# Gated mix of attention with memory and a gated feed-forward block: the last 256 output columns stored as two transfers, two weight loads issued in halves

## The chip, the cores and the metric

The kernel runs on one core of a Trainium2 chip. The metric is the device time of one execution in microseconds, the median of several runs. TensorE is called PE here, VectorE DVE, ScalarE ACT, GpSimd POOL and SyncE SP; SP issues nearly all DMA transfers.

## The reference

Sizes: 2048 tokens of width 512, 32 heads of 16, 4 segments of 512 tokens, 1792 hidden columns in the feed-forward block. All inputs and the output are bf16.

```python
def reference(A_x, A_wq, A_wk, A_wv, A_wo, A_beta, B_x, B_W_gate, B_W_up, B_W_down, gate_w):
    x = A_x
    g = _sigmoid((x * gate_w).sum(-1, keepdims=True))
    a = _A_ref(x, A_wq, A_wk, A_wv, A_wo, A_beta)   # attention in each segment + memory of the earlier ones, then @ wo
    b = _B_ref(x, B_W_gate, B_W_up, B_W_down)       # (relu(x @ W_gate) * (x @ W_up)) @ W_down
    return g * a + (1 - g) * b
```

## The kernel before, in words

The work goes over four segments of 512 tokens. For each segment `project` makes queries, keys and values, `attend` computes the scores, their exponentials and the attended values, `memory` adds to the running memory, and `ffn` computes the feed-forward block. `ffn` ends in 128-row pieces of output: 14 products with the down weight `wd_sb` (7 in a step named `D`, 7 in a step named `DB`) and 4 products with the output weight `wo_sb` (step `W`) go into one PSUM bank `rb`; a step `OS` scales the bank by the token's gate into an SBUF tile, on ACT or DVE; a step `ST` on SP stores it to HBM.

Every piece of work is a `Step` with an engine, a cost and the steps that it comes after. The order of the steps on each engine is written out in the table `ORDER`: each number is step number times 5 plus an index into `ENGINES` (PE, ACT, DVE, POOL, SP's queue), so the last digit's class names the engine, and only the order among numbers of one class matters. `lay_out` merges the five queues into one program; the framework then adds semaphore waits for data and for buffers.

The transfers of SP take eight semaphores in turn, DMAHW0 to DMAHW7. A transfer waits until the eighth transfer before it, which used the same semaphore, has landed. At the very end of the program SP waits for all of them and for the last steps of DVE and ACT, in five wait instructions of two semaphores each, in this order: (DMAHW3, DMAHW2), (DMAHW4, DMAHW1), (DMAHW5, DMAHW0), (DMAHW6, DVE), (DMAHW7, ACT). A barrier of all engines follows. The page shows all of these under line L1001.

The down weight (1792 KB, `ld["wd"]`, L363) and the output weight (512 KB, `ld["wo"]`, L364) are each loaded by one transfer through the helper `dma` (shown at L324).

The last 128 rows of the last segment are done by `last_rows` (L842) in three column groups: 256, 128 and 128 columns. Each has its own products (L852, L860) and its own scaling (L869 on ACT for the first two, L871 on DVE for the third). The scaled columns go into two 256-column tiles, `osbh[0]` and `osbh[1]` (named `rg` in the trace, because they are the first halves of two `rg` buffers). Two stores follow (L877): one for columns 0 to 255, issued after the first scaling, and one for columns 256 to 511, issued after the second and the third.

```python
            if h != 1:
                def sto(e, s, z=min(h, 1)):
                    nc.sync.dma_start(out=outf[tt * P:(tt + 1) * P, 2 * P * z:2 * P * z + 2 * P], in_=osbh[z])
                add(f"ST{seg}3", {"QSP": 0.4}, sto, after=dmas[-2:], prio=0.0)
```

Of the kernel before, what the change touches and what calls it, by code (L numbers as in the profile page):

```python
# [99 lines left out]
]  # L100
T0, TU, SPAN, PEN_D, PEN_A, PEN_P = 19.0, 15.6, 4.1, -23.0, 150.0, 146.0


PORT = {'TG', 'RN', 'RC', 'OA', 'KO', 'MB', 'MQ', 'MN', 'GS', 'PQ', 'PK', 'N1', 'N2', 'N3', 'NM'}
PIECE = {'MK': 0.445, 'TL': 0.22, 'ZE': 0.24, 'YL': 0.22, 'MB': 0.3}


class Step:
    pass

# [102 lines left out]
def kernel(  # L213
# [108 lines left out]
    def dma(eng, o, i, after=(), prio=0.0, kb=512, lat=3.0, name="dma"):  # L322
        key = {"SP": nc.sync, "ACT": nc.scalar, "POOL": nc.gpsimd}[eng]
        return add(name, {"Q" + eng: kb / 365.0}, lambda e, s: key.dma_start(out=o, in_=i),  # L324
                   after=[e_q, *after], prio=prio, lat=lat)

    def rows(ap, c0=None, c1=None):
        v = ap.rearrange("(c p) n -> p c n", p=P)
        return v if c0 is None else v[:, :, c0:c1]
# [676 lines left out]
```

## Time and profile before

| | |
|---|---|
| median of 3 runs | 266.98 us (266.53 to 267.01) |
| span of the profiled execution | 265.0 us |
| what the median has beyond that span | 1.98 us |
| PE busy | 258.1 us (97%) |
| ACT, DVE, POOL busy | 189.7, 181.0, 143.7 us |
| granted TensorE clock | 1.000 |
| HBM read, written | 8.26 MB, 2.10 MB |

The span runs from the first to the last instruction of the profiled execution. No other time of this execution is recorded, so the measured time of a run is set beside it: the start and end of an execution that the span leaves out are taken as the 1.98 us of the table. Busy times of different engines overlap and are not to be added.

### The profile page before, as it was taken

What the parts mean: (1) busy time and instruction counts of PE and PEld (TensorE: products, weight loads), DVE (VectorE), ACT (ScalarE), POOL (GpSimd) and SP (SyncE); (2) the same over time, 40 slices, a digit from 0 to 9 for tenths busy, and PEclk for the clock granted to TensorE, in tenths of its full rate; (3) what the DMA queues carried; (4) which work ended last, traced back from release to release, by engine and by line L of the source; (5) the groups of instructions that cost most, each with busy time, mean ns of one, the idle gap of its engine ahead of it and who ended that gap; (6) DMA issues with size and microseconds to landing.
All of it is one profiled execution on the core that took longest, in us unless ns stands there. A gap on an engine that the chain in (4) does not pass through costs nothing.

```text
span 265.0 us, 7943 instructions
## 1 busy us (share of the span) xinstructions
PE 258.1 (97%) x3293; PEld 121.0 (46%) x3337; DVE 181.0 (68%) x449; ACT 189.7 (72%) x185; POOL 143.7 (54%) x328
## 2 busy tenths in 40 slices
PE   7999999999999999999999999999999999999995
PEld 5444443545444444434444445454544444444554
DVE  1589788897774538855896476688878367666911
ACT  3699799987868786887777686886766576767012
POOL 8038978782826641378758464366468156064010
DMA  6978680426501000030403110000023100031002
GB/s 197 314 166 264 149 288 3 71 74 89 79 4 37 25 2 2 20 82 1 104 2 82 25 42 2 0 4 2 2 61 87 42 20 2 0 81 23 0 2 79
DMA packets 33422, 16.77 MB, mean 63 GB/s; under 512 B 20074, under 2 KB 33386, under 8 KB 33386
## 3 DMA queue, kind: packets, MB, share of 16 engines
q1 hardware_dynamic: 33098, 16.00, 24.3%
q8 instruction: 26, 0.43, 0.7%
q10 hardware_dynamic: 288, 0.26, 0.3%
q14 instruction: 10, 0.08, 0.1%
HBM read 8.26 MB, written 2.10 MB: 39 GB/s over the span
## 4 chain that ended last, share of the span: by engine, by line
PE 94%; DMA 1%; DVE 1%; issue 1%; ACT 1%; SPq 0%
PE rb L894 36%; PE rb L928 17%; PE rb L477 11%; PE sp L735 9%; PE rb L783 7%; PE rb L941 5%; PE rb L519 4%; DMA wv_sb<-in_A_wv_dram 1%; PE rb L678 1%; PE rb L852 1%; PE rb L502 1%; DVE hT L913 1%; ACT E L746 1%; PE rb L632 1%; PE rb L860 0%
## 5 line engine op out<-in xcount | busy, mean ns | idle before, releaser
L746 ACT ACTIVATE E<-sp 128x2048 bf16<-128x2048 f32 x72 | 135.1, 1877 | 35.0 <-PE sp L735 32.8
L756 POOL TENSOR_SCALAR_AFFINE_SELECT E<-E 64x256 bf16<-64x256 bf16 x256 | 112.3, 438 | 82.2 <-ACT E L746 68.7
L894 PE MATMUL rb<-xT,wg_sb 128*128 128x512 bf16 x216 | 55.4, 380 | 0.4
L894 PE MATMUL rb<-xT,wu_sb 128*128 128x512 bf16 x208 | 54.9, 380 | 0.8
L913 DVE TENSOR_TENSOR hT<-rb,rg 128x512 bf16<-128x512 f32 x56 | 38.2, 686 | 20.1 <-PE rb L894 14.1
L928 PE MATMUL rb<-wd_sb,hT 128*128 128x512 bf16 x198 | 48.6, 380 | 0.8 <-issue 0.2
L894 PEld LDWEIGHTS <-wg_sb 128*128 128x128 bf16 x224 | 20.7, 98 | 24.8 <-issue 3.1
L894 PEld LDWEIGHTS <-wu_sb 128*128 128x128 bf16 x224 | 20.1, 98 | 23.5 <-issue 4.5
L735 PE MATMUL sp<-QT,KT 16*64 16x320 bf16 (+7 forms) x512 | 30.3, 295 | 0.0
L735 PE MATMUL sp<-QT,KTo 32*64 32x320 bf16 (+7 forms) x512 | 30.3, 295 | 0.0
L928 PEld LDWEIGHTS <-hT 128*128 128x128 bf16 x210 | 19.4, 98 | 23.8 <-issue 3.2
L801 DVE STREAM_TRANSPOSE tA<-rb 128x512 f32<-128x512 f32 x32 | 21.9, 700 | 12.0 <-PE rb L783 11.6
L906 ACT ACTIVATE rg<-rb 128x512 bf16<-128x512 f32 x36 | 21.3, 598 | 10.1 <-PE rb L894 7.1
L735 PEld LDWEIGHTS <-KT 16*64 16x64 bf16 x512 | 10.5, 102 | 27.5 <-issue 26.9
L908 DVE TENSOR_SCALAR rg<-rb 128x512 bf16<-128x512 f32 x20 | 13.8, 688 | 7.5 <-PE rb L894 7.3
L783 PE MATMUL rb<-E,Vs 64*32 64x448 bf16 (+7 forms) x512 | 18.8, 284 | 0.0
L783 PE MATMUL rb<-E,Vp 64*32 64x448 bf16 (+7 forms) x512 | 18.4, 284 | 0.0
L950 ACT ACTIVATE osb<-rb,ngcol 128x512 bf16<-128x512 f32 x8 | 5.5, 691 | 16.2 <-PE rb L941 16.2
L952 DVE TENSOR_SCALAR osb<-rb,ngcol 128x512 bf16<-128x512 f32 x7 | 5.2, 750 | 16.1 <-PE rb L941 15.9
L477 PE MATMUL rb<-xT,wq_sb 128*128 128x512 bf16 x63 | 16.1, 380 | 0.0
L812 DVE TENSOR_TENSOR o<-tA,co 128x256 bf16<-128x256 f32 x32 | 15.4, 493 | 0.2
L477 PE MATMUL rb<-xT,wk_sb 128*128 128x512 bf16 x59 | 15.4, 379 | 0.2
(97 smaller groups left out, 298.3 us busy)
## 6 DMA issues: line engine op xcount, KB each, us to landing
out_dram<-osb SPq DMA_DIRECT2D x15, 128.0 KB, 1.8
wd_sb<-in_B_W_down_dram SPq DMA_DIRECT2D x1, 1792.0 KB
wg_sb<-in_B_W_gate_dram SPq DMA_DIRECT2D x3, 512.0 KB, 6.3
wu_sb<-in_B_W_up_dram SPq DMA_DIRECT2D x3, 512.0 KB, 6.0
Vs<-Vp SPq DMA_DIRECT2D x8, 144.0 KB, 3.2
wk_sb<-in_A_wk_dram SPq DMA_DIRECT2D x2, 256.0 KB, 3.9
wq_sb<-in_A_wq_dram SPq DMA_DIRECT2D x2, 256.0 KB, 4.7
wo_sb<-in_A_wo_dram SPq DMA_DIRECT2D x1, 512.0 KB, 4.2
```

What stands on the lines that cost most here:

```text
L477: nc.tensor.matmul(rb[s.bank][:], lhsT=w[:, ci, c * P:(c + 1) * P], rhs=xT[i][:, ci, :], start=(ci == 0), stop=(ci == NC - 1))
L735: nc.tensor.matmul(sp[64 * h:64 * h + 64, j, off:off + m], lhsT=kt[32 * j:hi, c0 + w, 64 * ck:64 * ck + 64], rhs=QT[i][32 * j:hi, c0 + w, ...
L746: nc.scalar.activation(Er[n % NE][:], sp[:], ACT.Exp, scale=SCALE)
L756: nc.gpsimd.affine_select(out=v, in_=v, compare_op=ALU.is_ge, fill=0.0, base=0, pattern=[[0, 4], [1, 64]], channel_multiplier=-1)
L783: nc.tensor.matmul(rb[s.banks[h]][32 * j:32 * j + 32, q0:q0 + m], lhsT=v[64 * h:64 * h + 64, ck // 2, o:o + 32], rhs=Er[(base + f) % NE][6 ...
L801: nc.vector.transpose(tA[k].rearrange("p b w -> p (b w)"), rb[a.banks[r]][:])
L812: nc.vector.tensor_tensor(o16[u % 2][:, :, r, :], tA[k][:, :, 0:DH], cos[k][:, :, None].to_broadcast([P, NB, DH]), ALU.mult)
L894: nc.tensor.matmul(rb[s.bank][:], lhsT=w[:, ci, fv * P:(fv + 1) * P], rhs=xT[i][:, ci, :], start=(ci == 0), stop=(ci == NC - 1))
L906: nc.scalar.activation(rgb[k][:], rb[a.bank][:], ACT.Relu)
L908: nc.vector.tensor_scalar(rgb[k][:], rb[a.bank][:], 0.0, None, ALU.max)
L913: nc.vector.tensor_tensor(hT[:, fv, :], rb[a.bank][:], rgb[k][:], ALU.mult)
L928: nc.tensor.matmul(rb[b][:], lhsT=hT[:, fv, lc:lc + P], rhs=wd_sb[:, fv, :], start=(fv == 0), stop=False)
```

## The change

Three edits. The stores of the last rows become three: columns 0 to 255 as before, columns 256 to 383 after the second scaling, and columns 384 to 511 after the third. The loads of the down and of the output weight are each issued as two transfers back to back inside the same step, the first half and the second half of the 128-row blocks of the weight. `ORDER` gets one number for the new store step (5544), and later numbers rise by 5; the three numbers at its head change places, but they belong to three different engines (79 SP, 81 ACT, 135 PE), so no engine's order changes by it.

```diff
-    79, 81, 135, 140, 160, 150, 146, 170, 167, 350, 157, 176, 355, 375, 380, 385, 390, 190, 180, 397, 360, 196, 365,
+    135, 81, 79, 140, 160, 150, 146, 170, 167, 350, 157, 176, 355, 375, 380, 385, 390, 190, 180, 397, 360, 196, 365,
...
+    def halves(eng, o, i, n, prio, kb):
+        a = dma(eng, o[:, 0:n], i[:, 0:n], prio=prio, kb=kb)
+        key = {"SP": nc.sync, "ACT": nc.scalar}[eng]
+
+        def both(e, s):
+            for h in range(2):
+                key.dma_start(out=o[:, h * n:h * n + n], in_=i[:, h * n:h * n + n])
+        a.emit = both
+        return a
...
-    ld["wd"] = dma("SP", wd_sb[:], rows(B_W_down), prio=7, kb=1792)
-    ld["wo"] = dma("SP", wo_sb[:], rows(A_wo), prio=8)
+    ld["wd"] = halves("SP", wd_sb[:], rows(B_W_down), NF // 2, 7, 1792)
+    ld["wo"] = halves("SP", wo_sb[:], rows(A_wo), NC // 2, 8, 512)
...
-            dmas.append(osl)
-            if h != 1:
-                def sto(e, s, z=min(h, 1)):
-                    nc.sync.dma_start(out=outf[tt * P:(tt + 1) * P, 2 * P * z:2 * P * z + 2 * P], in_=osbh[z])
-                add(f"ST{seg}3", {"QSP": 0.4}, sto, after=dmas[-2:], prio=0.0)
+            def sto(e, s, h=h, c0=c0, c1=c1):
+                nc.sync.dma_start(out=outf[tt * P:(tt + 1) * P, c0:c1],
+                                  in_=osbh[min(h, 1)][:, c0 % (2 * P):c0 % (2 * P) + c1 - c0])
+            add(f"ST{seg}3", {"QSP": 0.4}, sto, after=[osl], prio=0.0)
```

Between the two programs the line numbers differ by 11 or 12 from the helper on. Apart from line numbers and from the names of the DMA semaphores, which shift by up to three places, ACT, DVE and POOL have the same instructions in the same order. PE has the same instructions too, and two of its matmuls get a wait more.

SP's queue at the end of the program, before; `osb` and `rg` are the SBUF tiles that are stored, and what a transfer waits for stands in brackets:

```order
L336 DMA_TRANSPOSE memT<-mtok 128x4x128 [waits DMAHW7_49]
L955 DMA out_dram<-osb_150 128x512 [waits DMAHW0_49,DVE_49]
L955 DMA out_dram<-osb_149 128x512 [waits DMAHW1_49,Activation_49]
L955 DMA out_dram<-osb_151 128x512 [waits DMAHW2_49,Activation_49]
L877 DMA out_dram<-rg_146 128x256 [waits DMAHW3_49,Activation_49]
L877 DMA out_dram<-rg_147 128x256 [waits DMAHW4_49,DVE_49,Activation_49]
L1001 UNCONDITIONAL_BRANCH
```

The same place in the changed program:

```order
L348 DMA_TRANSPOSE memT<-mtok 128x4x128 [waits DMAHW1_49]
L966 DMA out_dram<-osb_150 128x512 [waits DMAHW2_49,DVE_49]
L966 DMA out_dram<-osb_149 128x512 [waits DMAHW3_49,Activation_49]
L966 DMA out_dram<-osb_151 128x512 [waits DMAHW4_49,Activation_49]
L887 DMA out_dram<-rg_146 128x256 [waits DMAHW5_49,Activation_49]
L887 DMA out_dram<-rg_147 128x128 [waits DMAHW6_49,Activation_49]
L887 DMA out_dram<-rg_147 128x128 [waits DMAHW7_49,DVE_49]
L1012 UNCONDITIONAL_BRANCH
```

One store has become two, and with two more transfers far ahead of it the last store now holds DMAHW7 where it held DMAHW4. The five closing wait instructions name the same pairs in the same order in both programs, so the last store's semaphore stands in the fifth of them and no longer in the second.

SP's queue where the down weight (`wd_sb`) and the output weight (`wo_sb`) are loaded, before; `pK` is the transposed key tile of the first segment:

```order
L324 DMA wd_sb<-in_B_W_down_dram 128x14x512 [waits DMAHW6_49]
L336 DMA_TRANSPOSE pK<-pkT_145 128x4x128 [waits DMAHW0_49,DMAHW7_49,DVE_49,PE_49]
L336 DMA_TRANSPOSE pK<-pkT_144 128x4x128
L324 DMA wo_sb<-in_A_wo_dram 128x4x512 [waits DMAHW1_49]
L336 DMA_TRANSPOSE pK<-pkT_144 128x4x128 [waits DMAHW2_49,DVE_49,PE_49]
```

And after:

```order
L335 DMA wd_sb<-in_B_W_down_dram 128x7x512 [waits DMAHW6_49]
L335 DMA wd_sb<-in_B_W_down_dram 128x7x512 [waits DMAHW7_49]
L348 DMA_TRANSPOSE pK<-pkT_145 128x4x128 [waits DMAHW0_49,DVE_49,PE_49]
L348 DMA_TRANSPOSE pK<-pkT_144 128x4x128 [waits DMAHW1_49]
L335 DMA wo_sb<-in_A_wo_dram 128x2x512 [waits DMAHW2_49]
L335 DMA wo_sb<-in_A_wo_dram 128x2x512 [waits DMAHW3_49]
L348 DMA_TRANSPOSE pK<-pkT_144 128x4x128 [waits DMAHW4_49,DVE_49,PE_49]
```

Each weight takes two places in the queue, ahead of the same transposes. The two matmuls of PE that get a wait more are the first to read the second half of each weight.

110 rows, old and new, of the table ORDER are left out of this document.

## The prediction

> **What bounds the kernel now.** I read the page's head and its chain of waits first, to see whether the middle of the program has room in which the two split weight loads could matter.
>
> ```profile
> span 265.0 us, 7943 instructions
> PE 258.1 (97%) x3293; PEld 121.0 (46%) x3337; DVE 181.0 (68%) x449; ACT 189.7 (72%) x185; POOL 143.7 (54%) x328
> PE 94%; DMA 1%; DVE 1%; issue 1%; ACT 1%; SPq 0%
> ```
>
> PE is busy for 97% of the span and makes 94% of the chain. Its instructions and their order stay as they are, so nothing between about 6 us and the last matmul can shrink by this change; it can only grow, where a weight came late. What is left is the tail behind the last matmul. I read it in the chain of waits from 261 us on, then in the timeline and in the lines of the two last stores (L877), of the scaling before them (L869) and of the closing waits (L1001).
>
> ```profile
> 261.82 0.24 PE rb L860 x4
> 262.08 0.35 DVE rg L871
> 262.49 0.33 SPq L877 DMA_DIRECT2D out_dram<-rg  x1
> L877 SPq EVENT_SEMAPHORE  x2: 17/352/687, 260.9 to 261.8; - x2
> DMA to landing us min/median/max: 1.5/1.5/1.5
> L1001 SPq EVENT_SEMAPHORE  x5: 28/28/28, 263.0 to 264.2; - x5
> SPq L1001 <- DMA out_dram<-rg: 1.0, 1, 1.0
> ```
>
> The last product ends at 262.06, DVE scales it by 262.43 (262.08 + 0.35), SP issues the last store at 262.49, and it lands 1.5 us later, at about 264.0. SP sits for 1.0 us in the closing waits for it. The span ends at 265.0. So the last 3 us hold a DVE step of 0.35, a store of 1.5 and a second of semaphores and barrier, one behind the other, with no engine working beside them. A saving there goes straight into the time, and a loss too.
>
> **The change part by part.** Durations come from the profiled execution, of 265.0 us from first to last instruction; the median of 266.98 has 1.98 us around that span, which I take as unchanged.
>
> First, the closing waits. The lines of L1001 on SP, asked for a stretch around the landing (263.9 to 264.3) and then for two narrow ones (264.02 to 264.05 and 264.21 to 264.24):
>
> ```profile
> L1001 SPq EVENT_SEMAPHORE  x4: 28/28/28, 264.0 to 264.2; - x4
> L1001 SPq EVENT_SEMAPHORE  x1: 28/28/28, 264.0 to 264.0; - x1
> L1001 SPq EVENT_SEMAPHORE  x1: 28/28/28, 264.2 to 264.2; - x1
> ```
>
> Of the five, one was done at 263.0; four run after the landing. The first of these four is the one that held DMAHW4, the last store's semaphore, and three more follow it, the fourth starting between 264.21 and 264.24, the first between 264.02 and 264.05: 0.16 to 0.22 us for three, so about 0.063 each. In the changed program the last store holds DMAHW7, which stands in the fifth wait. The four ahead of it ask for transfers that landed earlier, and the newest of those is the middle store. It can be issued when ACT has finished its second scaling:
>
> ```profile
> L869 ACT ACTIVATE rg<-rb,ngcol x2: 367/420/473, 260.9 to 261.5; 128x256 bf16<-128x256 f32 x1, 128x128 bf16<-128x128 f32 x1
> L877 SPq DMA_DIRECT2D out_dram<-rg x2: 332/332/332, 261.4 to 262.5; - x2
> ```
>
> The second scaling ends near 261.83 (261.46 + 0.37; the two together are 0.93 us from 260.90). The first store occupies SP until 261.73 (261.40 + 0.33). So the middle store issues at about 261.86 and lands by about 263.4, half a microsecond before the last one. The three waits are then over when the last store lands: **0.19 us** saved (0.16 to 0.22).
>
> Second, the issue of the last store. Before, one separate wait instruction of 687 ns on SP held DVE's semaphore and DMAHW4 together, and the store followed it: 262.49 against 262.43, 0.06 us after DVE ended. The first store has its data wait on the transfer itself and started at 261.40, where ACT ended at 261.37:
>
> ```profile
> 260.90 0.47 ACT L869 ACTIVATE rg<-rb,ngcol 128x256 bf16<-128x256 f32 x1 [0.58 <-PE rb L860]
> ```
>
> That is 0.03 us. The new last store waits only for DVE and DMAHW7, and like the first one it can carry the data wait itself: **0.03 us** saved. What could spoil it is SP's extra store ahead of it: issued at 261.86 it occupies SP until 262.19, and with some 0.1 us for the next wait SP stands ready at about 262.3, 0.13 us before DVE ends. So the cover holds; if ACT were late by 0.2 us, the last store would be late by 0.07.
>
> Third, the store itself becomes smaller: 128 rows of 256 bytes instead of 128 rows of 512. No store of this width is in the trace. Rows near to it are the stores of the page, by size, and the DMA share while the packets of the last store ran:
>
> ```profile
> out_dram<-osb SPq DMA_DIRECT2D x15, 128.0 KB, 1.8
> out_dram<-rg SPq DMA_DIRECT2D x2, 64.0 KB, 1.5
> Vs<-Vp SPq DMA_DIRECT2D x8, 144.0 KB, 3.2
> 260.30:261.90 1.60, 1.60 (x28) 1.52 (x25) 0.00 (x0) 0.86 (x3) 0.00 (x0) 1.00 0.72 246
> 263.20:263.70 0.50, 0.00 (x0) 0.00 (x0) 0.00 (x0) 0.00 (x0) 0.00 (x0) 1.00 0.44 131
> ```
>
> In the last row the 16 DMA engines are busy for 0.44 of 0.50 us, which is 0.22 us each for 8 rows of 512 bytes, 0.027 us a row. The row above moves 246 GB/s x 1.60 us = 394 KB at 1 KB a row, 385 rows or 24 for each engine, in 1.60 x 0.72 = 1.15 us: 0.048 a row. Carrying the line on, a row of 256 bytes takes 0.027 - 0.021 / 2 = 0.017 us, and 8 of them 0.13 instead of 0.22: 0.09 saved. From 128 KB to 64 KB the landing fell by 0.3, so half of that, 0.15, is what a size proportional to bytes gives. I take **0.10 us**, nearer to the packets' own time. The ends are a gain of 0.3 (the whole step from 1.8 to 1.5 once more) and a loss of 1.7 (if short rows make it as slow as the slowest short-row transfer of the page, Vs<-Vp with 3.2).
>
> The Trainium skill speaks against this part: the page DMA: Bandwidth & Descriptors, in its Specifications, puts the smallest transfer at line rate at 512 bytes, with a read-modify-write below it. No run here shows it yet, since all stores of this kernel have at least 512 bytes a row. By it the third term would be a loss and not a gain; two of the rivals are what that does.
>
> Fourth, the two split loads:
>
> ```profile
> 32.87 0.57 SPq L324 DMA_DIRECT2D wd_sb<-in_B_W_down_dram  x1
> 46.96 3.30 SPq L336 DMA_TRANSPOSE pK<-pkT  x2
> 50.31 0.58 SPq L324 DMA_DIRECT2D wo_sb<-in_A_wo_dram  x1
> 56.73 3.35 SPq L336 DMA_TRANSPOSE pK<-pkT  x2
> 38.00:40.00 2.00, 2.00 (x10) 0.77 (x8) 1.81 (x4) 2.00 (x4) 0.94 (x3) 1.00 0.88 309
> 40.00:42.00 2.00, 2.00 (x17) 0.92 (x17) 2.00 (x6) 1.57 (x2) 1.79 (x4) 1.00 0.00 1
> L928 PE MATMUL rb<-wd_sb,hT x198: 378/379/390, 63.4 to 255.9; 128*128 128x512 bf16 x198
> wo_sb<-in_A_wo_dram SPq DMA_DIRECT2D x1, 512.0 KB, 4.2
> L941 PE MATMUL rb<-wo_sb,oT x7: 379/379/389, 81.7 to 83.2; 128*128 128x512 bf16 x7
> ```
>
> Each adds one issue of 0.6 us to SP. Behind the down weight SP's next work starts at 46.96, 13.5 us after 33.44; behind the output weight at 56.73, 5.8 us after 50.89. Both issues vanish in these gaps; without the gaps they would cost the transposes of `pK` 0.6 us each. The down weight has landed by 40 (the DMA share falls from 0.88 to nothing) and is first read at 63.4; the output weight lands at 54.5 and is first read at 81.7. Twenty-three and twenty-seven microseconds cover any way of cutting them. On the critical engine two matmuls get a wait on a semaphore that has long been there. The batch at 81.7 begins with a matmul that already carries such a wait: its longest is 389 ns against a median of 379, so at most 0.01 us each; I take nothing, with 0.02 lost as the bound.
>
> The two transfers more also shift which transfer each later one has to wait for, but only to ones that landed long before. For instance the two transfers that follow the output weight and the transposes of `pK` (the third segment's input and the first load of `Vs`, in the 60s of the span) now ask for the halves of the down weight, landed by 40.
>
> Sum: 0.19 + 0.03 + 0.10 = **0.32 us** less, a span of 264.7 and a median of 266.98 - 0.32 = **266.66 us**, 0.12% less.
>
> **The rivals.** *The store's landing shrinks by a whole step.* If the fall from 1.8 to 1.5 repeats, the third term is 0.30 and the sum 0.52: 266.46, at the edge of 0.2%. For it speaks that the two page rows have only their size between them; against it, that the packets of the last store take 0.22 us in all, so more than that can't come from fewer bytes. Chance 0.15.
>
> *The short rows give the gain back.* If each row of 256 bytes takes another pass, a read and then a write, the packets' time of 0.22 doubles: the landing becomes 1.72, the third term a loss of 0.22, and the sum 0.19 + 0.03 - 0.22 = 0: 266.98. This is the mild form of the skill's rule above. Against it speaks that the line from 1024 to 512 bytes shows nothing but a smaller cost. Chance 0.13.
>
> *Slower: the last store waits for a slow write.* The mechanism is the same place, the one transfer that nothing covers, but with a full round trip to memory ahead of its writes, so that it lands like Vs<-Vp in 3.2 us instead of 1.5: 266.98 - 0.22 + 1.7 = 268.46. It decides as soon as the landing is over 1.5 + 0.22 + 0.53 = 2.25 us. Against it: rows of 512, 576 and 1024 bytes are all there, and Vs<-Vp differs by more than width (256 pieces on 64 partitions, between two SBUF tiles). Chance 0.06.
>
> That the change doesn't do what it says is not open: the order shows the last store on the fifth wait.
>
> **How the numbers follow.** A measurement of this kernel can tell about 0.2%, 0.53 us, from no change: the three runs before differ by 0.48. The forecast has the chance 0.66 that is left. Its own bounds are a third term of 0 to 0.15 and a first of 0.16 to 0.22: 266.58 to 266.83; the runs' spread, 0.24 to either side, widens that to 266.3 to 267.1. This holds the first two rivals as well, nearly whole, and I take 266.25 to 267.10. Faster by over 0.2% (below 266.45): 0.6 of the first rival and, by spread, 0.2 of the forecast, together 0.22. Slower (above 267.51): the third rival, 0.06, and 0.01 by spread: 0.07. Within 0.2%: 0.71.
>
> **What would show it.** In the profile after, the last store's DMAHW7 wait should be the only closing wait that ends after the landing, with one drain directly behind it. The middle store should issue at about 0.5 us after the first, the last at 0.03 us after DVE, and its landing should read 1.4. The first reads of both weights should start where they did, at 63.4 and 81.7, within 0.1. The forecast is wrong if the landing is over 1.6, if the last store issues after DVE by 0.1 or more, or if PE's last matmul ends over 0.3 us earlier or later than 262.06: then something in the middle moved, for which I have no cause.

## The result and the profile after

| | before | after |
|---|---|---|
| median | 266.98 us (266.53 to 267.58, 17 runs) | 266.58 us (266.31 to 267.29 and one of 299.43, 17 runs) |
| after to before | | 0.9984, 95% interval 0.9976 to 0.9992 |

The change saves 0.16%, 0.4 us, with an interval from 0.2 to 0.6 us. The run of 299.43 us, the profiled one, had a granted clock of 0.853; ratio and interval leave it out, and the lines below come from a second profile of the same program at full clock (run *again* below). First the head of its page and its chain of waits at the end, which answer to the lines shown of before:

```profile
span 265.6 us, 7945 instructions
PE 259.0 (98%) x3293; PEld 121.6 (46%) x3337; DVE 181.0 (68%) x449; ACT 189.7 (71%) x185; POOL 143.8 (54%) x328
```

```profile
262.60 0.24 PE rb L872 x4
262.84 0.02 issue
262.86 0.35 DVE rg L883
```

This span is longer than that of before, 265.6 against 265.0, and its last product ends at 262.84 instead of 262.06. So PE's last product lies 0.78 us later in this execution, and the tail behind it is shorter. The two have to be read apart. The tail first: its timeline, the lines of the last stores (now L887), of the closing waits on SP (now L1012, asked for three stretches) and the sizes of the transfers.

```profile
262.18 1.39 SPq L887 DMA_DIRECT2D out_dram<-rg  x3
```

```profile
L887 SPq EVENT_SEMAPHORE  x3: 17/17/17, 261.7 to 263.0; - x3
L887 SPq DMA_DIRECT2D out_dram<-rg x3: 332/333/350, 262.2 to 263.2; - x3
DMA to landing us min/median/max: 1.5/1.5/1.5
```

```profile
L1012 SPq EVENT_SEMAPHORE  x3: 28/28/28, 263.6 to 263.8; - x3
L1012 SPq EVENT_SEMAPHORE  x1: 28/28/28, 264.1 to 264.1; - x1
...
L1012 SPq EVENT_SEMAPHORE  x1: 28/28/28, 264.7 to 264.7; - x1
L1012 SPq DRAIN  x1: 13/13/13, 264.8 to 264.8; - x1
```

```profile
out_dram<-rg SPq DMA_DIRECT2D x2, 32.0 KB, 1.5
```

The separate wait (EVENT_SEMAPHORE) in front of the last store is 17 ns instead of 687: the store holds its data wait itself and starts at 263.24, 0.03 us after DVE's end at 263.21. Three of the closing waits are over at 263.8, the fourth at 264.1, when the middle store has landed, and only the fifth runs at 264.72, when the last store has; the drain, SP's next instruction, follows it at 264.78. Before, the drain came 0.25 us after the first wait behind the landing (264.29 against 264.04):

```profile
L1001 SPq DRAIN  x1: 7/7/7, 264.3 to 264.3; - x1
```

### The profile page after: what moved, and what is told of

It reads as the page before. It is cut to its first block, busy times and chain, and to the rows that moved or that the text cites. A ratio compares the mean times of both kernels' runs of the same rounds, so it can differ in the third digit from the quotient of the medians.

```text
span 297.7 us, 7945 instructions
## 1 busy us (share of the span) xinstructions
PE 290.2 (97%) x3293; PEld 128.3 (43%) x3337; DVE 180.9 (61%) x449; ACT 191.0 (64%) x185; POOL 143.9 (48%) x328
## 4 chain that ended last, share of the span: by engine, by line
PE 96%; issue 1%; DMA 1%; DVE 1%; DVEq 0%
PE rb L905 38%; PE rb L939 18%; PE rb L489 11%; PE sp L747 9%; PE rb L795 7%; PE rb L952 5%; PE rb L531 4%; PE rb L514 1%; PE rb L690 1%; PE rb L864 1%; DMA xT<-in_A_x_dram 1%; PE rb L644 1%; PE rb L402 1%; PE rb L872 0%; DVE hT L924 0%
## 5 line engine op out<-in xcount | busy, mean ns | idle before, releaser
L905 PE MATMUL rb<-xT,wg_sb 128*128 128x512 bf16 x216 | 63.0, 421 | 0.6
L905 PE MATMUL rb<-xT,wu_sb 128*128 128x512 bf16 x208 | 61.9, 420 | 1.2
L939 PE MATMUL rb<-wd_sb,hT 128*128 128x512 bf16 x198 | 55.5, 420 | 1.1 <-issue 0.2
L905 PEld LDWEIGHTS <-wg_sb 128*128 128x128 bf16 x224 | 22.2, 104 | 29.8 <-issue 3.3
L905 PEld LDWEIGHTS <-wu_sb 128*128 128x128 bf16 x224 | 21.5, 104 | 27.6 <-issue 4.7
L795 PE MATMUL rb<-E,Vs 64*32 64x448 bf16 (+7 forms) x512 | 20.8, 303 | 0.0
L795 PE MATMUL rb<-E,Vp 64*32 64x448 bf16 (+7 forms) x512 | 20.4, 304 | 0.0
L489 PE MATMUL rb<-xT,wq_sb 128*128 128x512 bf16 x63 | 18.1, 416 | 0.0
L489 PE MATMUL rb<-xT,wk_sb 128*128 128x512 bf16 x59 | 17.5, 423 | 0.3
L952 PE MATMUL rb<-wo_sb,oT 128*128 128x512 bf16 x58 | 16.3, 422 | 0.2
```

Source lines behind the costliest of these rows:

```text
L489: nc.tensor.matmul(rb[s.bank][:], lhsT=w[:, ci, c * P:(c + 1) * P], rhs=xT[i][:, ci, :], start=(ci == 0), stop=(ci == NC - 1))
L795: nc.tensor.matmul(rb[s.banks[h]][32 * j:32 * j + 32, q0:q0 + m], lhsT=v[64 * h:64 * h + 64, ck // 2, o:o + 32], rhs=Er[(base + f) % NE][6 ...
L905: nc.tensor.matmul(rb[s.bank][:], lhsT=w[:, ci, fv * P:(fv + 1) * P], rhs=xT[i][:, ci, :], start=(ci == 0), stop=(ci == NC - 1))
L939: nc.tensor.matmul(rb[b][:], lhsT=hT[:, fv, lc:lc + P], rhs=wd_sb[:, fv, :], start=(fv == 0), stop=False)
L952: nc.tensor.matmul(rb[hold.bank][:], lhsT=oT[i][:, ci, lc:lc + P], rhs=wo_sb[:, ci, :], start=False, stop=(ci == NC - 1))
```

## The experiments

Runs of the same program differ in when PE begins its long middle part, so two distances are compared besides the times: from the first product with the down weight to the last product of the program (the middle), and from the end of DVE's last step to the end of the span (the tail). All are from the records of the profiled executions, in microseconds. For stores_only and loads_only the landing of the last store is not recorded; it is read from the closing wait that it ends, which in the others starts 0.02 us after the landing.

| kernel | first down product | middle | tail | landing of the last store | waits behind it | time to before, 95% interval |
|---|---|---|---|---|---|---|
| before | 63.40 | 198.42 | 2.62 | 1.53 | 3 | 1 |
| again | 64.19 | 198.42 | 2.34 | 1.46 | 0 | 0.9987 (0.9972 to 1.0002) |
| again2 | 63.65 | 198.42 | 2.34 | 1.46 | 0 | 0.9991 (0.9981 to 1.0000) |
| stores_only | 63.88 | 198.42 | 2.43 | 1.44 | 2 | 0.9988 (0.9976 to 1.0000) |
| loads_only | 63.37 | 198.43 | 2.50 | 1.53 | 1 | 0.9997 (0.9986 to 1.0009) |
| pad_only | 63.39 | 198.42 | 2.45 | 1.53 | 0 | 0.9990 (0.9981 to 1.0000) |
| first_wait | 63.16 | 198.42 | 2.61 | 1.49 | 4 | 1.0000 (0.9988 to 1.0012) |
| last64 | 63.61 | 198.50 | 2.61 | 1.46 | 0 | 0.9987 (0.9978 to 0.9997) |
| warm24 | 63.94 | 198.51 | 2.32 | 1.46 | 0 | 0.9994 (0.9983 to 1.0005) |

**The changed kernel twice more** (no edit).

> The changed kernel itself, for a profile at full clock and a second comparison. Theory (only the tail moved): PE's last matmul ends within 0.1 us of the 262.06 of before; the last store issues 0.03 us after DVE ends (before 0.06), lands 1.47 us later (before 1.53 to 1.55), and only one closing wait ends after the landing. Span 264.7 to 264.8, time 0.30 us under before. Rival (the split loads moved the middle): PE's last matmul ends more than 0.1 us earlier than 262.06, and the tail accounts for less than the whole gain.

> The changed kernel once more, beside warm24 on the same chip. Theory: 0.28 us under before (2.62 - 2.34 behind DVE's end), ratio 0.999, and the first down product anywhere between 63.1 and 64.2, with 198.42 us from it to the last product. Rival (something in the middle moved after all): that distance differs by more than 0.02.

The tail came out as the theory has it both times: 2.34 us instead of 2.62, a gain of 0.28. The middle is 198.42 us, the same as before to the last digit. What failed is the expectation on the place of the last product: it lies 0.78 and 0.25 us later than before. Since the middle is unchanged, that shift arises ahead of the first down product, and it is there in kernels that are alike in that part of the program; the last experiment turns to it. The span of 264.7 was therefore missed (265.6 and 265.0). The times are 0.13% and 0.09% under before, but both intervals reach no change, so these two runs alone do not show the gain; that of the result does.

**The stores alone.** Both weights are loaded whole:

```diff
-    ld["wd"] = halves("SP", wd_sb[:], rows(B_W_down), NF // 2, 7, 1792)
-    ld["wo"] = halves("SP", wo_sb[:], rows(A_wo), NC // 2, 8, 512)
+    ld["wd"] = dma("SP", wd_sb[:], rows(B_W_down), prio=7, kb=1792)
+    ld["wo"] = dma("SP", wo_sb[:], rows(A_wo), prio=8)
```

> The three stores alone; both weights are loaded by one transfer each as before. The last store then holds DMAHW5, the third of the five closing waits. Theory: two waits of 0.063 us follow the landing, so 0.06 of the 0.19 us of the first term is left, with 0.04 from the earlier issue and 0.07 from the smaller store: 0.17 us under before, and from DVE's end to the span's end 2.44 us (2.615 before). Rival (the middle carries the gain): as fast as the changed kernel in the tail, and at the time of before where the loads mattered.

The closing waits of this kernel between 264.3 and 264.6, the landing being at 264.37:

```profile
L1012 SPq EVENT_SEMAPHORE  x3: 28/28/28, 264.4 to 264.5; - x3
```

The first of the three holds the last store, two follow, and the tail is 2.43 against 2.44 expected. Without the two split loads the smaller store gives only 0.19 of the 0.28 us.

**The loads alone.** Before, with the two weights in halves and the two stores as they were:

```diff
-    ld["wd"] = dma("SP", wd_sb[:], rows(B_W_down), prio=7, kb=1792)
-    ld["wo"] = dma("SP", wo_sb[:], rows(A_wo), prio=8)
+    ld["wd"] = halves("SP", wd_sb[:], rows(B_W_down), NF // 2, 7, 1792)
+    ld["wo"] = halves("SP", wo_sb[:], rows(A_wo), NC // 2, 8, 512)
```

> The two split loads alone, with the two stores of before. The last store (256 columns) then holds DMAHW6, the fourth closing wait. Theory: one wait follows the landing, two fewer than before: 0.13 us under before, all behind the landing; issue 0.06 us after DVE and landing 1.53 as before; PE's last matmul within 0.1 us of 262.06. Rival (the split loads move the middle): a gain of 0.2 us or more, and PE's last matmul earlier by that.

Its closing waits from 263.9 to 264.1:

```profile
L1011 SPq EVENT_SEMAPHORE  x2: 28/28/28, 264.0 to 264.1; - x2
```

One wait follows the landing; the tail is 2.50, 0.12 less than before, and issue and landing are those of before (0.06 and 1.53). The middle, which begins with the first use of the split weight, did not move. The loads themselves are issued ahead of it, at 33 to 51 us; the stretch from PE's first product with `wk_sb` (8 to 9 us) to the first down product, which holds them, took 55.15 us here, 55.13 in before, and 55.13 in the seven others. The time itself, 0.9997 with 0.1% to either side, can't tell 0.12 us from none; the tail can.

**Other counts of transfers.** *pad_only* is before with the down weight in two and the output weight in three transfers, so that the old store comes to the fifth wait; *first_wait* is the changed kernel with both weights in four transfers, so that the new store comes to the first. With a helper `parts_of` that issues the pieces between given cuts (the helper and the lines replaced are left out here):

```diff
# pad_only, against before
+    ld["wd"] = parts_of("SP", wd_sb[:], rows(B_W_down), (0,7,14), 7, 1792)
+    ld["wo"] = parts_of("SP", wo_sb[:], rows(A_wo), (0,2,3,4), 8, 512)
# first_wait, against the changed kernel
+    ld["wd"] = parts_of("SP", wd_sb[:], rows(B_W_down), (0,4,7,11,14), 7, 1792)
+    ld["wo"] = parts_of("SP", wo_sb[:], rows(A_wo), (0,1,2,3,4), 8, 512)
```

> The two stores of before, with the down weight loaded in two and the output weight in three transfers: three transfers more, so that the last store (256 columns, behind a joint wait) holds DMAHW7, the fifth closing wait, as in the changed kernel. Theory (the closing waits carry two thirds of the gain): from DVE's end to the span's end 2.615 - 0.19 = 2.43 us; the issue (0.06 after DVE) and the landing (1.53) stay as before; 0.19 us under before. Rival (the smaller store carries the gain): 2.6 us and the time of before.

> The changed kernel with both weights cut into four transfers instead of two, so that four transfers more shift the last store's semaphore to DMAHW3, the first of the five closing waits. Theory: four waits follow the landing, 4 x 0.063 = 0.25 us more than in the changed kernel; against before the earlier issue (0.04), the smaller store (0.07) and one wait more (0.06) leave 0.05 us under before. Rival (finer loads help the middle): at least as fast as the changed kernel.

The closing waits behind the landing, of pad_only (263.9 to 264.1) and of first_wait (263.6 to 264.03):

```profile
L1011 SPq EVENT_SEMAPHORE  x1: 28/28/28, 264.0 to 264.0; - x1
```

```profile
L1022 SPq EVENT_SEMAPHORE  x5: 28/28/28, 263.7 to 264.0; - x5
```

In pad_only nothing but the place of the semaphore differs from before at the end of the program, and the tail is 2.45 against 2.62 (2.43 expected). The drain comes 0.08 us after the landing instead of 0.27; 0.02 of this is lost again behind the drain. In first_wait all five waits run after the landing, and the whole gain of the smaller store is gone: 2.61, 0.27 more than in the changed kernel (0.25 expected), and a time equal to before. So the closing waits are priced at both ends, 0.06 us for each that stands behind the landing, and cutting the loads finer shows no effect of its own.

**A still smaller last store.** The changed kernel with

```diff
-        outs, dmas, cuts = [], [], (0, 2 * P, 3 * P, D)
+        outs, dmas, cuts = [], [], (0, 2 * P, 3 * P + 64, D)
```

> The changed kernel with the last columns cut 256, 192 and 64 instead of 256, 128 and 128, so that the last store has rows of 128 bytes. Theory on the store (a row costs 0.009 us per 256 bytes less, whatever the width): it lands in 1.43 us instead of 1.46, and DVE's step takes 0.28 instead of 0.35, so the part behind the last matmul shrinks by 0.10. Rival on the store (short rows take another pass below some width): it lands later than 1.5. On PE: if a product with 64 columns takes half of one with 128 (0.055 us), the whole is 0.10 us faster than the changed kernel; if the weight load behind each product keeps it at 0.055, the 18 products of the middle group grow from 0.055 to 0.082 with nothing back, 0.48 us, and the whole is 0.38 us slower than the changed kernel, 0.08 slower than before.

The DMA share while the packets of the last store ran, in *again* (rows of 256 bytes) and in *last64* (rows of 128 bytes), then the end of last64's timeline:

```profile
264.00:264.50 0.50, 0.00 (x0) 0.00 (x0) 0.00 (x0) 0.00 (x0) 0.00 (x0) 1.00 0.30 66
```

```profile
263.70:264.10 0.40, 0.00 (x0) 0.00 (x0) 0.00 (x0) 0.00 (x0) 0.00 (x0) 1.00 0.27 41
```

```profile
262.34 0.28 DVE L883 TENSOR_SCALAR rg<-rb,ngcol 128x64 bf16<-128x64 f32 x1 [2.56 <-PE rb L872]
...
262.93 0.38 SPq L887 DMA_DIRECT2D out_dram<-rg  x1
```

Busy time of each DMA engine for its 8 rows: 0.22 us at 512 bytes (before), 0.50 x 0.30 = 0.15 at 256 and 0.40 x 0.27 = 0.11 at 128. It falls steadily; nothing like another pass appears. But the step expected to gain lost. DVE is done at 262.62, and the last store starts 0.31 us later, at 262.93, because SP was still issuing the middle store: that one could start only when ACT had scaled 192 columns (done at 262.44), and from 262.47 it held SP for 0.38. The cover of 0.13 us that the prediction found in front of the last store is used up and turned into a wait. PE's side was the cheap case: from start to start a product with 64 columns took 0.029 us and one with 128 (in before) 0.056, and the last product came 0.02 us later, measured from the first output-weight product of the program, not 0.48. (In this kernel and in warm24 another 0.06 and 0.09 us of the middle were lost ahead of that product, which no run explains.) The landing, 1.46 with 0.05 more in the issue, did not get shorter in sum. By the trace this kernel is 0.27 us behind the changed one in the tail, 2.61; from the first down product to the end of the span it takes 201.62 us, against 201.64 before and 201.37 in again, so it should be about as fast as before. Its time is 0.13% under before (0.03 to 0.22%), and no run explains this gap.

**Where the runs' spread comes from.** The changed kernel with `NWARM = 24` instead of 19.

> The changed kernel with 24 instead of 19 empty products on PE at the start, which fill the 0.3 us in which PE waits for the first rows of x. It asks whether the spread of the runs, which lies ahead of the first down product, comes from PE running at half rate there. Theory (the half rate ends at a moment that does not depend on this gap): no change in the mean, at most 0.1 us slower where x had landed already; 266.6 to 266.8 with the spread of before. Rival (the gap puts off the full rate): the slow starts go away, the runs lie closer together and the mean falls by 0.2 to 0.4 us under the changed kernel, 0.5 to 0.7 under before.

The first products with `wv_sb` on PE between 4.3 us and 6.2 us, by their line, with min, median and max in ns. In before (to 5.1 us), where the first down product came at 63.40, and in first_wait (63.16):

```profile
L502 PE MATMUL rb<-wv_sb,xT x4: 379/379/389, 4.4 to 5.0; 128*128 128x512 bf16 x4
```

```profile
L524 PE MATMUL rb<-wv_sb,xT x6: 376/379/389, 4.3 to 5.8; 128*128 128x512 bf16 x6
```

In again (64.19) and in warm24 (63.94):

```profile
L514 PE MATMUL rb<-wv_sb,xT x5: 609/634/634, 4.5 to 6.2; 128*128 128x512 bf16 x5
```

```profile
L514 PE MATMUL rb<-wv_sb,xT x5: 610/634/634, 4.5 to 6.1; 128*128 128x512 bf16 x5
```

The engines in the stretch from 4.4 to 6.3 us, of before and of again; the first number behind the length is PE's busy time, and the third column from the end is the granted clock:

```profile
4.40:6.30 1.90, 1.64 (x8) 0.46 (x6) 0.25 (x2) 0.37 (x1) 1.72 (x2) 1.00 0.89 259
```

```profile
4.40:6.30 1.90, 1.90 (x8) 0.73 (x6) 0.37 (x2) 0.39 (x2) 1.72 (x2) 1.00 0.86 259
```

The same products take 379 ns in one execution and 634 in another. From start to start it is 0.216 us in before and 0.427 in again. All nine executions begin at the slow pace: from 1.04 us on, products with 128 columns follow each other at 0.107 us, and later at 0.055. What differs is the moment of the change.

The clock column does not show it, because it counts time without a record as full. The traces of before and of first_wait have no record of the clock at all (so the 1.000 of before says only that no lower clock was recorded), and in again the one record within the span, at full clock, begins at 7.31 us. In the others it begins at 4.61 (pad_only), 5.55 (loads_only), 5.94 (again2), 6.01 (last64), 6.46 (stores_only) and 6.60 us (warm24). In each of the seven, PE's products go over from the slow to the fast pace at that moment; in before and first_wait they do so between 4.1 and 4.4 us. Where the change is late, everything behind lies later: the first product with `wk_sb` comes at 8.48 to 9.05 us in the five executions with a change after 5.9, and at 8.03 to 8.27 in the four others. From there to the first down product all nine agree to 0.03 us, so the whole shift arises in the first 9 us.

Five more empty products, which close PE's gap before the first rows of x, changed nothing that shows: the change came at 6.60, among the others, and the mean of the runs is 266.85 (266.35 to 267.59) against 266.80 and 266.76 in the two series of the changed kernel. So the rival falls, and the theory stands as far as it goes; what sets the moment was not varied. The record at full clock lasts 259.41 us in each of the seven, though its start moves by 2.7 us; that fits a rhythm that does not follow the program, but does not prove it. The Trainium skill, in TensorE: Matmul & The Clock Gate, Part 1, has 426.7 and 215.7 ns for the cold and the warm array at 512 columns, and a window that runs free of the kernel's start and moves the change from one to the other by half a microsecond to either side. The trace agrees in both durations; the change moved further here, over some 3 us, and that the window is the cause no run here shows.

## Why the prediction was right, point by point

**The closing waits**, 0.19 predicted, were 0.19 from the landing to the drain, and 0.17 of the tail, in the one kernel that moves nothing else (pad_only), and follow the count of waits behind the landing, from 0 to 4, in every kernel whose last store was not held up otherwise. The drain came 0.27 us after the landing before and 0.08 after the change, 0.19 apart.

**The issue of the last store**, 0.03 predicted: 0.064 us after DVE's end before, 0.028 in the changed kernel, 0.036 saved. SP's middle store did not hold it up, since it was issued 0.60 us ahead.

**The smaller store**, 0.10 predicted with ends from a gain of 0.3 to a loss of 1.7: 1.53 to 1.46, 0.07 saved (the other last stores with 256-byte rows landed in 1.44 to 1.49). That is the packets' own time and no more: it fell from 0.22 to 0.15, where the prediction's line gave 0.13. Both rivals that rested on slow short rows fall with it. The Trainium skill's page DMA: Bandwidth & Descriptors has, under Specifications, line rate only from 512 bytes and a read-modify-write below. These stores agree with the first half: a DMA engine's 8 rows moved 19, 14 and 9 bytes per ns at 512, 256 and 128 bytes. Of the second half they show no cost, since 8 rows of 256 and of 128 bytes took less time than 8 of 512; the loss that the prediction drew from it did not come. The first rival, another 0.3 us, falls too. The reading of 1.4 that the prediction named came out as 1.46, which the page rounds to 1.5.

**The split loads**, nothing predicted: in the kernels that change only stores and loads, the middle of 198.42 us is the same to 0.01 with one, two, three or four transfers for a weight, and the stretch ahead of it in which the loads are issued is the same to 0.03. The only effect seen is on which closing wait the last store falls.

The terms measured add up to 0.19 + 0.04 + 0.07 = 0.30, and the tails differ by 0.28, where 0.32 was predicted; 0.015 of the difference lies behind the drain (0.77 us to the end instead of 0.75). The timed gain is 0.40 with an interval of 0.2 to 0.6; the runs can't say whether more than the tail moved, and the equal middles give no room for it there. That 266.58 lies so near to the forecast of 266.66 is in part luck, since single runs of one kernel differ by about a microsecond, and the range of 266.25 to 267.10 held the time of before as well. It is the terms, measured one by one, that bear the forecast out.

**What was wrong** is the test that the prediction set itself: that a last product over 0.3 us off 262.06 would mean that something in the middle moved. It was 0.78 us off in one execution, and the middle had not moved; the start had, as it does from one execution to the next. The first reads of the two weights, expected within 0.1 us of 63.4 and 81.7, came at 64.19 and 82.47 for the same reason. The prediction took the spread of the three runs as given and did not ask where in the program it arises.

Two smaller slips change nothing in the forecast. In every run the time is 1.7 to 1.8 us above the span, so the 1.98 us of the table of before sets the median beside an execution that was itself about 0.3 us faster than the median. And the upper end of the forecast's own bounds, 266.83, does not follow from its terms: 0.16 + 0.03 saved and 0.02 lost at the loads give 266.81.

## What to carry to other kernels

At the end of a program like this one, after the last store lands, everything left is serial: count the wait instructions that stand behind the last transfer's semaphore, since with semaphores dealt out in turn their number depends on how many transfers were issued anywhere before. A transfer added far ahead under full cover could change the end of this program by 0.06 us a place, in either direction. And for changes below the runs' spread, compare distances between two events of the same execution, chosen so that the source of the spread lies outside them.

## What the runs showed of the hardware that was not expected

- A closing wait whose semaphores are long there still costs 0.06 us, 28 ns of it as its own duration.
- A wait on two semaphores in an instruction of its own delayed the store behind it by 0.064 us after the event; a wait for DVE on the store itself, behind a separate wait that was long over, by 0.028.
- Rows of 512, 256 and 128 bytes to HBM took each DMA engine 0.22, 0.15 and 0.11 us for 8 of them; the whole landing was 1.53, 1.46 (1.44 to 1.49 in other executions) and 1.46 us, so most of it does not depend on size.
- PE's products ran at half the pace at the start of all nine executions (0.107 us instead of 0.055 from one to the next at 128 columns, and 0.427 instead of 0.216 at 512), up to a moment between 4.1 and 7.3 us that differed from one to the next. Where the trace has a record of the full clock, it begins at that moment; the clock column reads 1.00 ahead of it too, because nothing is recorded there.
